# A gated-memory attention with a feed-forward layer on one core: two steps of a chunk run shifted, in three bursts of small products

## The chip, the cores and the metric

The kernel runs on one core of a Trainium2 chip. The time is that of the device from the first to the last instruction of the program, in microseconds (us). A core has a matrix engine (TensorE, PE in the profile; its weight loads are shown apart as PEld), a vector engine (VectorE, DVE), a scalar engine (ScalarE, ACT), GpSimd (POOL) and DMA queues (most of them issued by SyncE, SP). The matrix engine writes into PSUM, from where VectorE and ScalarE take the results.

## What is computed

A DeltaNet attention over 4 batches, 8 heads, 768 positions and 48 dimensions, followed by a feed-forward layer of 3072 tokens, 384 to 2048 to 384, with a PReLU between the two products. All is in float32.

```python
# attention, per batch and head; k_n is k divided by its norm
for t in range(S):
    kt, vt, bt = (k_n[:, :, t], v[:, :, t], beta[:, :, t, None])
    y[:, :, t] = np.einsum('bhd,bhde->bhe', q[:, :, t], state)
    v_old = np.einsum('bhde,bhd->bhe', state, kt)
    state = state + bt[:, :, :, None] * np.einsum('bhd,bhe->bhde', kt, vt - v_old)
# ... y becomes x, one row of 384 per token, and then
h = x @ w_in
g = np.maximum(h, 0.0) + alpha * np.minimum(h, 0.0)
out = g @ w_out
```

## The kernel before

The 768 positions are cut into 12 chunks of C = 64. A chunk is worked on in two steps of two batches each (16 matrices: 8 heads, two batches one above the other on the 128 partitions), so there are N = 24 steps; step n belongs to chunk n // 2. NJ is 4, G is 4 (pairs of heads), D is 48. Within a chunk the recurrence is solved by the inverse of a triangular 64 x 64 matrix per head and batch. Its two 32 x 32 blocks on the diagonal are inverted by elimination on VectorE, four steps (two chunks) at a time, and the part between them comes from two rounds of products (`between_1`, `between_2`).

```python
def flip(src, p):                       # q or k to the other side, two heads at a time
    for g in range(G):
        nc.tensor.transpose(
            p[:, g * 128 : (g + 1) * 128],
            src[:, 2 * g : 2 * g + 2].rearrange("p h d -> p (h d)"),
            ident,
        )
# heads lie 64 apart in src (48 values and 16 zeros each), so columns 112 to 127 are zeros

def grams(n):                           # k k^T of a later step
    p = ps_big()[:, :, 0 : G * C].rearrange("p a (g i) -> p a g i", g=G)
    for g, a, t in quarters():          # 16 products
        nc.tensor.matmul(
            p[half(t), a, g], k_t[n][dims(a), g, half(t)], k_t[n][dims(a), g, half(t)]
        )
    # ... two weighted evacuations by VectorE, into the blocks for elimination and into right[n]

def eliminate(m):                       # a generator: 39 or 43 pieces, each some VectorE operations
    # ... for j in range(1, HB - 1): prod = r * r; r = r + prod; yield

def through_state(n):
    p = ps_big()[:, :, 0 : G * (D + C)].rearrange("p a (g e) -> p a g e", g=G)
    for g, a, t in quarters():
        nc.tensor.matmul(
            p[half(t ^ a), a, g], k_t[n][dims(a), g, half(t)], beside[bp][dims(a), t, g]
        )
    p_y = ps_big()[:, :, 0 : G * D].rearrange("p a (g d) -> p a g d", g=G)
    for g, a, t in quarters():
        nc.tensor.matmul(
            p_y[half(t), a, g], q_t[n][dims(a), t, g], state[bp][dims(a), t, g]
        )
    # ... r = v - p by VectorE in three operations, the masked products of q and k, y by ScalarE
```

`solve` multiplies the inverse by r and gives u; `outputs` adds the masked products times u to y; `next_state` subtracts k times u from the state. Each of these, and of `between_1` and `between_2`, is 16 products of 48 to 64 rows and columns into a buffer of its own, followed at once by its evacuation. `ps_big` has three buffers of two banks of PSUM each; two more banks, `ffn_banks`, are the feed-forward layer's, used in turn.

One step of the attention, and how it is put among the products of the feed-forward layer:

```python
def attention(n):
    place(n + 1, (0,))
    through_state(n)
    between_1(n + 1)
    yield
    solve(n)
    grams(n + EARLY)
    between_2(n + 1)
    scale_v(n + 1)
    yield
    outputs(n)
    next_state(n)
    load_late(n + 2)
    squares(n + EARLY + 1)
    yield
    flips(n + EARLY + 1, n + 2)
    to_ffn(n)
    # ... loads of later steps
    yield

for n in range(NJ, N):
    gens = [(attention(n), SHARES), (placing(n + 1, (1, 2, 3)), SHARES * PLACING)]
    if n % NJ == 0 and n < N - NJ:
        m = n // NJ + 1
        blocks, left = eliminate(m), WHOLE + (PIECES if m > 2 else 0)
        share = -(-left // 3)
    if n % NJ < 3 and n < N - NJ:
        gens.append((part(blocks, share), share))
    if n < NJ + 2:
        gens.append((part(late, (OUT_PARTS - few) // 2), (OUT_PARTS - few) // 2))
    else:
        parts = IN_PARTS - 4 if n % 2 == 0 else FAST_PARTS + 4
        gens.append((part(tail, parts), parts))
    # ... sums of weights in steps 5, 6 and 7
    weave(*gens)
```

`weave` deals the pieces of several generators into one order of issue, evenly by the numbers given; each engine then works in that order. The feed-forward layer's two parts:

```python
def ffn_in(c):                          # 48 pieces of one product each
    for f in range(0, FT, 2):
        # ... 6 products of 256 columns into one of the two banks (L840)
        nc.scalar.activation(g, p_h, ACT.Relu, scale=-1.0)               # L850
        for i in range(2):
            nc.vector.scalar_tensor_tensor(                              # L852
                out=g[:, i], in0=g[:, i], scalar=al_t[:, f + i : f + i + 1], in1=p_h[:, i],
                op0=ALU.mult, op1=ALU.add,
            )
        # ... sums of operands for the second layer by VectorE (L794)

def ffn_out_fast(c):                    # 28 pieces of two products each
    # ... 7 groups of 8 products of 192 columns (L904), each evacuated by L924
```

Lines that the profile names: 355 transposes of q and k, 392 `grams`, 399 its evacuations, 477 and 483 elimination, 641 `between_1`, 656 `between_2`, 682 and 687 `through_state`, 707 `solve`, 720 `outputs`, 736 `next_state`, 742 the state's update, 751 transposes of y.

Of the kernel before, what the change touches and what calls it, by code (L numbers as in the profile page):

```python
# [28 lines left out]
ALU = mybir.AluOpType  # L29
# [12 lines left out]
def kernel(  # L42
# [50 lines left out]
    NXT = 2  # L93

# [258 lines left out]
    def flip(src, p):  # L353
        for g in range(G):
            nc.tensor.transpose(  # L355
                p[:, g * 128 : (g + 1) * 128],
                src[:, 2 * g : 2 * g + 2].rearrange("p h d -> p (h d)"),
                ident,
            )

    def flips(n_k, n_q):
# [13 lines left out]
        for dst, src in copies:  # L375
            nc.scalar.copy(dst.rearrange("p g i -> p (g i)"), src)  # L376
        if n_q < N:
            nc.scalar.copy(  # L378
                q_t[n_q].rearrange("p t g i -> p g t i"),
                p_q.rearrange("p (g t i) -> p g t i", g=G, t=2),  # L380
            )
# [4 lines left out]
    def grams(n):  # L386

        if n >= N:
            return
        p = ps_big()[:, :, 0 : G * C].rearrange("p a (g i) -> p a g i", g=G)  # L390
# [5 lines left out]
        for dst, cols in (  # L396
            (gather(n), slice(0, HB)), (right[n % EARLY][:, 1:], slice(HB, C))
        ):
# [4 lines left out]
        keep(n)  # L403
# [231 lines left out]
    def between_1(n):  # L635

        if n >= N:
            return
        p = ps_big()[:, :, 0 : G * HB].rearrange("p a (g i) -> p a g i", a=2, g=G)
        for g, a, t in quarters():  # L640
# [5 lines left out]
        nc.scalar.copy(  # L646
            mid[n % 2].rearrange("p (a g) i -> p a g i", a=2)[:, :, :, 0:HB], p
        )

    def between_2(n):  # L650
        if n >= N:
            return
        p = ps_big()[:, :, 0 : G * HB].rearrange("p a (g i) -> p a g i", a=2, g=G)
# [8 lines left out]
        nc.vector.tensor_tensor(out=to, in0=to if changes(n) else own, in1=p, op=ALU.add)  # L662
# [12 lines left out]
    def through_state(n):  # L675
        c, bp = steps[n]
        if c == 0:
            rhs_[n] = by_parity(nv[n])
            return
        p = ps_big()[:, :, 0 : G * (D + C)].rearrange("p a (g e) -> p a g e", g=G)  # L680
# [4 lines left out]
        p_y = ps_big()[:, :, 0 : G * D].rearrange("p a (g d) -> p a g d", g=G)  # L685
# [7 lines left out]
        for to, own, a in (  # L693
            (slice(0, 128), slice(0, 128), 0), (half(0), half(1), 1), (half(1), half(0), 1)
        ):
# [3 lines left out]
        masked(n, p[:, :, :, D : D + C])  # L699
        y = work.tile([128, H, D], FP32, name="y")  # L700
        nc.scalar.copy(by_parity(y), p_y)  # L701
        rhs_[n], ys[n] = r, y

    def solve(n):
        p = ps_big()[:, :, 0 : G * D].rearrange("p a (g d) -> p a g d", a=2, g=G)
# [5 lines left out]
        nc.vector.tensor_tensor(  # L711
            out=us[n], in0=p,
            in1=stats[n][1][:, 0:3:2, :, None].to_broadcast([128, 2, G, D]), op=ALU.mult,
        )

    def outputs(n):
        c, bp = steps[n]
        p = ps_big()[:, :, 0 : G * D].rearrange("p a (g d) -> p a g d", a=2, g=G)
# [4 lines left out]
        if c == 0:  # L723
            ys[n] = work.tile([128, H, D], FP32, name="y")
            nc.scalar.copy(by_parity(ys[n]), p)
        else:
            nc.vector.tensor_tensor(
                out=by_parity(ys[n]), in0=by_parity(ys[n]), in1=p, op=ALU.add
            )

    def next_state(n):
        c, bp = steps[n]
        if c < NCH - 1:
            p = ps_big()[:, :, 0 : G * D].rearrange("p t (g d) -> p t g d", g=G)
# [5 lines left out]
            for a in range(2):  # L740
                x = state[bp][dims(a)]
                nc.vector.tensor_tensor(out=x, in0=x, in1=p[dims(a)], op=ALU.subtract)

# [231 lines left out]
    SHARES = 4  # L975

    def attention(n):


        place(n + 1, (0,))  # L980
        through_state(n)
        between_1(n + 1)
        yield
        solve(n)
        grams(n + EARLY)
        between_2(n + 1)
        scale_v(n + 1)
        yield
        outputs(n)
        next_state(n)  # L990
# [331 lines left out]
```

## Time and profile before

| | |
|---|---|
| median of three runs | 686.55 us (684.96 to 688.63) |
| span of the profiled execution | 683.6 us |
| TensorE busy | 660.0 us, 97% |
| VectorE busy | 471.3 us, 69% |
| ScalarE busy | 249.4 us, 36% |
| products of the feed-forward layer's first part (L840) | 1152 records, 268.8 us |

The page cuts the span into 40 slices and gives each engine's busy share in tenths. TensorE has single slices below 8 only at the very start; PEclk, the granted clock of TensorE, is full in all slices. The chain of work that ended last spends 79% of the span on TensorE, 13% on VectorE and 3% on ScalarE. A matrix product in float32 appears in the trace as two records, a transpose as one. The groups by line give the busy time of a group (overlapping records counted once), the mean length of a record and the idle time of the engine ahead of it.

### The profile page before, as it was taken

To read this page: it belongs to the slowest core of one execution; us is meant where nothing else is said; L and a number is where in the kernel's file an instruction comes from. 1 tells how busy PE (TensorE), PEld (TensorE's weight loads), DVE (VectorE), ACT (ScalarE), POOL (GpSimd) and SP (SyncE) were. 2 spreads that over 40 slices of the span, in tenths; PEclk is the share of its full clock that TensorE was granted. 3 is DMA by queue.
4 is the path that set the end of the run, shared out by engine and by line. 5 is a ranking of instruction groups with operands and counts; after the bars stand their busy time and mean duration, and the time that the engine had idled before them with its cause. 6 is when DMAs were issued, how large, how long until landed. Compare 5 with 4: busy or idle time off the path is not lost.

```text
span 683.6 us, 21618 instructions
## 1 busy us (share of the span) xinstructions
PE 660.0 (97%) x9359; PEld 570.2 (83%) x9359; DVE 471.3 (69%) x1162; ACT 249.4 (36%) x586; POOL 27.8 (4%) x95
## 2 busy tenths in 40 slices
PE   5989999999889999999999999999999999999997
PEld 4567777666678988988988988988989989989997
DVE  4966789879998379978479978379877255345261
ACT  4836756344434234235235235134034133231110
POOL 5000121000000000000000000000000000000000
PEclk9999999999999999999999999999999999999999
DMA  8847644211402112112112202201201211100000
GB/s 126 236 116 218 166 106 117 70 36 37 83 18 43 34 40 48 34 39 47 35 40 36 36 25 36 37 25 36 47 18 33 53 24 20 36 1 2 23 1 24
DMA packets 110958, 37.68 MB, mean 55 GB/s; under 512 B 104160, under 2 KB 107248, under 8 KB 110864
## 3 DMA queue, kind: packets, MB, share of 16 engines
q1 hardware_dynamic: 109088, 35.81, 24.0%
q8 instruction: 74, 1.21, 0.7%
q10 hardware_dynamic: 1776, 0.49, 0.4%
q14 instruction: 20, 0.16, 0.1%
HBM read 31.56 MB, written 4.72 MB: 53 GB/s over the span
## 4 chain that ended last, share of the span: by engine, by line
PE 79%; DVE 13%; ACT 3%; issue 1%; DMA 1%; SPq 1%; POOL 0%; ACTq 0%; DVEq 0%
PE p_ffn L840 32%; PE p_ffn L904 27%; PE p_big L355 3%; DVE block L483 2%; DVE prod L477 2%; PE p_big L682 2%; PE p_big L720 2%; PE p_big L707 2%; PE p_big L641 2%; PE p_big L1009 2%; DVE act L852 1%; PE p_big L656 1%; PE p_big L392 1%; PE p_big L687 1%; DMA ke<-in_k_dram 1%
## 5 line engine op out<-in xcount | busy, mean ns | idle before, releaser
L840 PE MATMUL p_ffn<-xt,w_in 128*128 128x256 f32 x1152 | 268.8, 385 | 6.2 <-DVE act L852 2.4
L840 PEld LDWEIGHTS p_ffn<-xt,w_in 128*128 128x128 f32 x1152 | 211.9, 190 | 37.0 <-issue 4.0
L852 DVE SCALAR_TENSOR_TENSOR act<-act,al_t,p_ffn 128x256 f32<-128x256 f32 x176 | 76.3, 475 | 56.8 <-ACT act L850 55.8
L850 ACT ACTIVATE act<-p_ffn 128x512 f32<-128x512 f32 x88 | 52.4, 596 | 129.7 <-PE p_ffn L840 120.1
L904 PE MATMUL p_ffn<-w_out,act 128*128 128x192 f32 x480 | 84.2, 329 | 0.3 <-DVE act L852 0.3
L904 PEld LDWEIGHTS p_ffn<-w_out,act 128*128 128x128 f32 x480 | 78.5, 190 | 1.9 <-DVE act L852 0.9
L483 DVE TENSOR_TENSOR block<-block,prod 128x30 f32<-128x30 f32 (+9 forms) x150 | 49.8, 332 | 5.2
L477 DVE TENSOR_TENSOR prod<-block 128x30 f32<-128x30 f32 (+9 forms) x150 | 48.9, 326 | 2.0
L924 DVE TENSOR_TENSOR o_sb<-u,p_ffn 128x192 f32<-128x192 f32 x40 | 13.2, 352 | 41.4 <-PE p_ffn L904 35.1
L378 ACT COPY beside<-p_big 128x512 f32<-128x512 f32 x24 | 14.0, 589 | 54.2 <-PE p_big L355 54.2
L376 ACT COPY k_t<-p_big 128x512 f32<-128x512 f32 x24 | 13.9, 580 | 51.6 <-PE p_big L355 51.5
L701 ACT COPY y<-p_big 128x384 f32<-128x384 f32 x22 | 10.5, 478 | 57.3 <-PE p_big L687 57.3
L904 PE MATMUL p_ffn<-space_out,sums 128*128 128x192 f32 x160 | 29.3, 326 | 0.0
L904 PE MATMUL p_ffn<-more,sums 128*128 128x192 f32 x160 | 29.3, 326 | 0.0
L696 DVE TENSOR_TENSOR r<-v_raw,p_big 64x192 f32<-64x192 f32 (+1 forms) x66 | 23.2, 352 | 7.3 <-PE p_big L682 6.2
L904 PE MATMUL p_ffn<-w_out,sums 128*128 128x192 f32 x160 | 27.7, 326 | 0.0
L904 PEld LDWEIGHTS p_ffn<-space_out,sums 128*128 128x128 f32 x160 | 26.6, 190 | 0.0
L904 PEld LDWEIGHTS p_ffn<-more,sums 128*128 128x128 f32 x160 | 26.6, 190 | 0.0
L441 ACT COPY same<-right 32x256 f32<-32x256 f32 x29 | 11.7, 402 | 40.1 <-DVE right L399 39.9
L904 PEld LDWEIGHTS p_ffn<-w_out,sums 128*128 128x128 f32 x160 | 25.8, 190 | 0.0
L924 DVE TENSOR_TENSOR u<-u,p_ffn 128x192 f32<-128x192 f32 x20 | 7.1, 354 | 26.4 <-PE p_ffn L904 26.3
L609 ACT ACTIVATE diag<-inverse,which 64x128 f32<-64x128 f32 (+2 forms) x60 | 24.2, 405 | 2.2 <-DVE inverse L453 1.3
(156 smaller groups left out, 948.5 us busy)
## 6 DMA issues: line engine op xcount, KB each, us to landing
w_out<-in_moe_w_in_dram SPq DMA_DIRECT2D x12, 512.0 KB, 5.0
qp<-in_q_dram SPq DMA_DIRECT2D x48, 96.0 KB, 2.9
v_raw<-in_v_dram SPq DMA_DIRECT2D x48, 96.0 KB, 2.9
kl<-in_k_dram SPq DMA_DIRECT2D x96, 48.0 KB, 2.4
out_dram<-o_sb SPq DMA_DIRECT2D x92, 48.0 KB, 1.6
space_out<-in_moe_w_out_dram SPq DMA_DIRECT2D x11, 384.0 KB, 4.3
ke<-in_k_dram SPq DMA_DIRECT2D x43, 96.0 KB, 3.1
w_out<-in_moe_w_out_dram SPq DMA_DIRECT2D x5, 384.0 KB, 3.6
```

What stands on the lines that cost most here:

```text
L355: nc.tensor.transpose(p[:, g * 128 : (g + 1) * 128], src[:, 2 * g : 2 * g + 2].rearrange("p h d -> p (h d)"), ident,)
L376: nc.scalar.copy(dst.rearrange("p g i -> p (g i)"), src)
L378: nc.scalar.copy(q_t[n_q].rearrange("p t g i -> p g t i"), p_q.rearrange("p (g t i) -> p g t i", g=G, t=2),)
L477: nc.vector.tensor_tensor(out=prod, in0=r[:, 0:j, j : j + 1].to_broadcast([128, j, n]), in1=r[:, j : j + 1, j + 1 : HB].to_broadcast([128, ...
L483: nc.vector.tensor_tensor(out=r[:, 0:j, j + 1 : HB], in0=r[:, 0:j, j + 1 : HB], in1=prod, op=ALU.add)
L609: nc.scalar.mul(out, x, which[rows, i : i + 1])
L696: nc.vector.tensor_tensor(out=r[to, a], in0=v_in[to, a], in1=p[own, a, :, 0:D], op=ALU.subtract)
L840: nc.tensor.matmul(p_h[:, i], w_in[:, t, (f + i) * 128 : (f + i + 1) * 128], xt[:, t], start=(t == 0), stop=(t == KT - 1),)
L850: nc.scalar.activation(g, p_h, ACT.Relu, scale=-1.0)
L852: nc.vector.scalar_tensor_tensor(out=g[:, i], in0=g[:, i], scalar=al_t[:, f + i : f + i + 1], in1=p_h[:, i], op0=ALU.mult, op1=ALU.add,)
L904: nc.tensor.matmul(p, x(i), w(i), start=(i == 0), stop=(i == FP - 1))
L924: nc.vector.tensor_tensor(out=to, in0=x, in1=p, op=ALU.add)
```

## The change

The steps of a chunk, an even one (e) and an odd one (o), no longer run one after the other but shifted by a part. What each of the two needs next is put into a common burst: three bursts per chunk instead of three per step. The products of a burst share buffers of PSUM (each takes a range of columns), and their evacuations are no longer issued with the products but handed back as a list of small functions, which `lasting` and `weave` spread over the feed-forward products that follow. `between_1` and `between_2` of a step move to earlier bursts. The transposes of q and k load 112 columns, leaving out the zeros at the end, and write 112 partitions; the copies behind them and the filling products `busy` follow suit. The elimination of the diagonal blocks is dealt over both chunks that it is for, where it stood in three of four steps. It is for TensorE: fewer changes between small and full products, smaller loads, and a more even VectorE.

```diff
+    ROWS = C + D
     def flip(src, p):
         for g in range(G):
             nc.tensor.transpose(
-                p[:, g * 128 : (g + 1) * 128],
-                src[:, 2 * g : 2 * g + 2].rearrange("p h d -> p (h d)"),
+                p[0:ROWS, g * 128 : (g + 1) * 128],
+                src[:, 2 * g : 2 * g + 2].rearrange("p h d -> p (h d)")[:, 0:ROWS],
                 ident,
             )
 ...
-    def solve(n):
-        p = ps_big()[:, :, 0 : G * D].rearrange("p a (g d) -> p a g d", a=2, g=G)
+    def solve(n, p=None):
+        p = region(p, G * D, g=G)
         for g, a, t in quarters():
             nc.tensor.matmul(
                 p[half(t ^ a), a, g], inv[n % NE][half(t), a * G + g], rhs_[n][half(t), a, g]
             )
         us[n] = work.tile([128, 2, G, D], FP32, name="u")
-        nc.vector.tensor_tensor(
+        return [lambda: nc.vector.tensor_tensor(
             out=us[n], in0=p,
             in1=stats[n][1][:, 0:3:2, :, None].to_broadcast([128, 2, G, D]), op=ALU.mult,
-        )
+        )]
 ... (the other products likewise)
-    def attention(n):
- ...
+    WY = G * D
+    def ends(n, p):
+        return outputs(n, p[:, :, 0:WY]) + next_state(n, p[:, :, WY : 2 * WY])
+
+    def burst_1(c):
+        e, last = 2 * c, 2 * c - 1
+        pieces = []
+        b = ps_big()
+        if e < N:
+            p, y = ps_big(), ps_big()
+            pieces += through_state(e, p[:, :, 0 : G * (D + C)], y[:, :, 0:WY])
+            pieces += between_2(e, b[:, :, 2 * WY : 2 * WY + G * HB])
+            pieces.append(lambda: load_v(e + 3))
+        if last > NJ:
+            pieces += ends(last, b)
+            pieces.append(lambda: load_late(last + 2))
+        return pieces
+
+    def burst_2(c):
+        e, o = 2 * c, 2 * c + 1
+        b, p, y = ps_big(), ps_big(), ps_big()
+        pieces = solve(e, b[:, :, 0:WY])
+        pieces += through_state(o, p[:, :, 0 : G * (D + C)], y[:, :, 0:WY])
+        pieces += between_2(o, b[:, :, WY : WY + G * HB])
+        pieces += grams(e + EARLY, y[:, :, WY : WY + G * C])
+        pieces += [lambda: load_v(o + 3), lambda: squares(o + EARLY)]
+        return pieces
+
+    def burst_3(c):
+        e, o = 2 * c, 2 * c + 1
+        a, b = ps_big(), ps_big()
+        pieces = solve(o, a[:, :, 0:WY])
+        pieces += between_1(o + 2, a[:, :, WY : WY + G * HB])
+        pieces += ends(e, b)
+        pieces += between_1(e + 2, b[:, :, 2 * WY : 2 * WY + G * HB])
+        pieces += grams(o + EARLY)
+        pieces += [lambda: load_late(e + 2), lambda: squares(e + EARLY + 2)]
+        return pieces
 ...
     def prelude(n):
         place(n)
+        place(n + 1, (0,))
         yield
-        between_1(n)
+        now(between_1(n))
+        now(between_1(n + 1))
         yield
-        between_2(n)
+        scale_v(n)
         yield
-        scale_v(n)
+        now(burst_1(n // 2))
         yield
 ...
-    for n in range(NJ, N):
- ...
+    def stretch(n, blocks, share, *gens):
+        gens = list(gens) + [(part(tail, n), n), (part(blocks, share), share)]
+        weave(*[x for x in gens if x[1] > 0])
+    def lasting(pieces, n):
+        return each(pieces), n * len(pieces)
+    SHORT, LONG = (4, 4, 3, 3, 3, 3), (13, 15, 15, 13, 10, 10)
+    SHARES = {2: (2, 3, 3, 3, 4, 4), 3: (6, 7, 7, 4, 5, 5)}
+    EVEN, ODD = (2, 2, 3, 4, 5, 5), (0, 4, 4, 4, 5, 5)
+    for c in range(2, NCH):
+        e, o = 2 * c, 2 * c + 1
+        count = SHORT if c == 2 else LONG
+        share = SHARES.get(c, ODD if c % 2 else EVEN)
+ ...
+        stretch(count[0], blocks, share[0], (placing(o, (1, 2, 3)), 8))
+        pieces = burst_2(c)
+        stretch(count[1], blocks, share[1], lasting(pieces, 2), *early_sums)
+        turn_2(c)                       # transposes of k and q, norms, loads
+        stretch(count[2] - 2, blocks, share[2])
+ ... (in odd chunks the elimination of the next two chunks begins here)
+        place(e + 2, (0,))
+        place(o + 2, (0,))
+        stretch(2, blocks, 0)
+        pieces = burst_3(c)
+        n = count[3] // 2
+        stretch(n, blocks, 0 if c % 2 else share[3] // 2, lasting(pieces, 1))
+        stretch(
+            count[3] - n, blocks, share[3] if c % 2 else share[3] - share[3] // 2, *late_sums
+        )
+        to_ffn(e)
+        scale_v(e + 2)
+        stretch(count[4], blocks, share[4], (placing(e + 2, (1, 2, 3)), 7))
+        pieces = burst_1(c + 1)
+        stretch(count[5], blocks, share[5], lasting(pieces, 2))
+        turn_1(c + 1)                   # transposes of k, q and y, norms, loads
```

## The prediction, made before the changed kernel was timed

> **What bounds the kernel now.** First the page's busy rows, to find the engine, then the busy time by stretch, to find where it is the bound.
>
> ```profile
> PE 660.0 (97%) x9359; PEld 570.2 (83%) x9359; DVE 471.3 (69%) x1162; ACT 249.4 (36%) x586; POOL 27.8 (4%) x95
> ```
>
> ```profile
> 150.00:217.00 67.00, 61.19 (x1103) 46.20 (x1100) 60.49 (x151) 29.03 (x75) 2.94 (x10) 1.00 0.26 49
> 217.00:250.00 33.00, 33.00 (x509) 31.02 (x508) 18.81 (x41) 11.03 (x30) 0.41 (x2) 1.00 0.19 38
> 250.00:650.00 400.00, 399.65 (x5334) 364.21 (x5333) 266.92 (x646) 123.27 (x288) 3.04 (x14) 1.00 0.16 31
> ```
>
> The columns after the stretch and its length are TensorE, its weight loads, VectorE, ScalarE and GpSimd. From 217 us to the end TensorE never stops (399.65 of 400.00 us): there a microsecond taken off its stream is a microsecond off the time, and a microsecond taken off VectorE (267 of 400) is worth nothing. From 150 to 217 us, which holds chunk 2 and half of chunk 3, TensorE is idle for 5.8 us and VectorE is busy for 60.5 of 67: VectorE is nearly the bound there.
>
> Busy is not the same as useful, so next the chain of work in order of time, one step of the attention in the steady part. Its columns are start, length (from the end of the piece before) and the number of records; an issued product shows as two records, a transpose as one.
>
> ```profile
> 300.26 0.44 PE p_big L656 x32
> 300.70 5.38 PE p_ffn L840 x24
> 306.07 0.61 PE p_big L720 x32
> 306.69 0.36 PE p_big L736 x32
> 307.05 4.95 PE p_ffn L840 x22
> 311.99 0.87 PE p_big L355 x8
> 312.87 0.33 PE p_big L751 x3
> 313.19 4.32 PE p_ffn L840 x20
> 317.51 0.93 PE p_big L682 x32
> 318.44 0.45 PE p_big L687 x32
> ```
>
> The reader is to compare pieces of one line by what stands before them. L840 after transposes: 4.32 us for 20 records, 0.216 each. L840 after small products: 5.38 for 24, where 24 x 0.216 is 5.18, and 4.95 for 22, where 22 x 0.216 is 4.75. So the return from small products to full ones costs 0.20 us, and the return from transposes nothing. The way in costs too: L720, first of its burst, takes 0.61 us; L656 and L687, which also load 64 columns per record but follow other small products, take 0.44 and 0.45. That is 0.15 us or more. One burst of small products costs **0.35 us beside the products in it**, whatever it holds.
>
> [...] all small products here work on 48 or 64 rows and columns, and 0.35 us is lost around each burst of them, none around transposes, which use all 128 rows. [...]
>
> ```profile
> L720 PEld LDWEIGHTS p_big<-u,a_t 64*64 64x64 f32 x384 | 6.7, 134 | 3.3 <-issue 3.1 <-DVE prod L477 0.2
> L736 PEld LDWEIGHTS p_big<-u,kl 64*48 64x48 f32 x384 | 5.5, 122 | 0.0
> ```
>
> 16 columns less make a load 12 ns shorter, and in the chain L736 (48 columns loaded) takes 0.36 us where groups with 64 columns take 0.44. [...]
>
> **The change, part by part.**
>
> *Bursts.* Before, each of the 20 steps from 4 to 23 has three bursts (state products with the first half of the next step's inverse; solve, Gram products and second half; outputs and new state), so 60, and the prelude has two: 62. After, the prelude has two (both first halves; burst 1), and each of the 10 chunks three: 32. The products are the same. 30 bursts less at 0.35 us are 10.5 us of TensorE time. Not all of it stands on the path: about 24 of the 30 lie after 217 us, 24 x 0.35 = **8.4 us**. The other 6 (2.1 us) fall into the stretch where VectorE is close to full; I count a third, **0.7 us**.
>
> *Transposes.* 188 of q and k load 112 columns in place of 128. 92 of them (60 of q, 32 of k by the line's count) come after 217 us. At 12 to 13 ns each that is 1.2 us, if the load sets the pace. If streaming does, it is nothing: L840 moves 256 columns in 0.216 us, so 128 columns at that rate would take 0.108 us, also what is seen. The trace of before can't tell. I take two chances in three, **0.8 us**. The copies behind them keep their 512 elements per partition and take what they took.
>
> *Inversion spread.* In chunks 2 and 3, elimination runs 13 blocks per step over three steps; after, 19 blocks stand in chunk 2 and 20 in chunk 3. So chunk 2 has 7 blocks (of some 0.8 us of VectorE) less, and chunk 3 up to its deadline 7 more. Total VectorE work up to the deadline near 217 us is unchanged, so little of the 5.8 us of idle TensorE can come back: I take **1.0 us**, since the waits for u and y in chunk 2 (0.4 and 1.5 us) should go. After 217 us TensorE doesn't wait and spreading is worth nothing by itself.
>
> *What is added.* No instruction. But evacuations of five or six products now come in one packet, and two banks of the feed-forward must be freed among them. After burst 3 of an even chunk VectorE has, between one pair of L852 and the next: one update of the state 0.55, two elimination pairs 0.8 each, L399 twice 0.41, an operand sum 0.69, a norm 0.55: 4.2 us. With 0.6 for the relu, 0.87 for the first pair and 0.48 for the first half of the second, the last operand of the second layer is ready 6.15 us after the burst's own bank is full. TensorE comes to need it after 12 records of 0.216 and 14 of 0.1625: 4.9 us. That would be a new wait of 1.2 us, in chunks 4, 6 and 8; in odd chunks the elimination is not there and it fits. Three such waits are 3.7 us; my order of work on VectorE is from the program, the moments are not, so I take less than half, **minus 1.5 us**.
>
> Sum: 8.4 + 0.7 + 0.8 + 1.0 - 1.5 = 9.4 us; 686.55 - 9.4 = 677.2, which I round to **677.0 us**.
>
> **The rivals.** (a) *The waits eat the gain.* A burst of 3 us with three double buffers of PSUM at once, products of one burst in the same banks, and packets of eight VectorE operations[...]. For it: the reckoning above, where the slack of a feed-forward bank is only about 1 us (2.6 us to fill the other one, less 0.6 and 0.87). Against: VectorE is full to 67% in the steady part, and before the change its packets of u, two Gram evacuations, the inverse and v (0.55 + 0.41 + 0.41 + 0.41 + 0.55) already stood in the same way, with only 0.35 us of idle TensorE in 400. A wait of 1.2 us in each of nine chunks would leave the time near 682.
> (b) *The cost of a burst is not fixed but goes with its length or the kinds in it.* A longer burst changes between products with different rows and columns more often. Then merging saves less, perhaps only the 0.20 us on the way out: 24 x 0.2 and the small terms make 681. Against: L687 after L682 and L656 after L392 show no extra.
> (c) *VectorE's stretch gains more than I give.* All of its 5.8 us of idle time and the whole of the 2.1 us there come back, and transposes pay in full: 671. For it: the shares of elimination look chosen for that stretch. Against: 60.5 us of VectorE work in 67.
>
> **Range and chances.** The firm part is 8.4 us, good to 15% (0.30 to 0.40 us a burst). The soft terms run from minus 4 (rival a) to plus 6 (rival c). The range is 671.5 to 682.5 us. Over 2% would need 672.8, so 13.7 us: only rival (c) nearly whole gets there, one chance in ten. Slower by over 2% would need 23 us of new waits; 0.02. Within 2%: 0.88.
>
> **What would show it.** In the chain after, full products behind transposes should keep 0.216 us, and those behind a burst carry 0.20 more, with three such places in a chunk instead of six; L700 (the old L682), where it is second in burst 2, should take about 0.78 us in place of 0.93. Eight transposes of k and q should take 0.77 us if loads set the pace, 0.87 if streaming does. Idle TensorE from about 217 us to the end should be under 4 us, and stand at L932 for act. If it is above 6, rival (a) is right; if a burst's overhead grows with its length, rival (b). The prediction fails if the number of bursts is not what sets that 0.35 us.

## The result, and the profile after

The changed kernel takes **707.08 us** (706.32 to 711.49, median of 4 runs); the kernel before, run beside it, takes 685.94. The ratio is **1.032 [1.027, 1.036]**: slower by 3%, where 677.0 was predicted, and outside the range of 671.5 to 682.5.

The row of busy time of the changed kernel:

```profile
PE 658.8 (94%) x9359; PEld 573.0 (81%) x9359; DVE 466.6 (66%) x1162; ACT 247.8 (35%) x586; POOL 29.5 (4%) x95
```

The numbers of instructions are the same on every engine, and the busy times changed by less than 5 us. So nothing was added to the work; TensorE stands idle for longer. Where, the busy time by stretch tells (columns as in the prediction; the last four are the granted clock, the DMA share and GB/s, after GpSimd):

```profile
150.00:194.00 44.00, 36.23 (x725) 25.51 (x726) 34.85 (x89) 19.31 (x53) 3.12 (x8) 0.92 0.28 52
194.00:217.00 23.00, 19.71 (x239) 16.73 (x239) 19.93 (x51) 7.91 (x19) 0.41 (x2) 1.00 0.27 52
217.00:250.00 33.00, 31.13 (x499) 28.94 (x498) 26.32 (x65) 9.71 (x24) 0.00 (x0) 1.00 0.11 22
250.00:650.00 400.00, 383.70 (x5321) 351.93 (x5320) 255.98 (x621) 123.55 (x295) 4.53 (x16) 1.00 0.16 31
```

From 250 to 650 us TensorE was idle for 0.35 us before and is now for 16.3. From 150 to 217 it is idle for 11.1 us in place of 5.8, and for once its clock was not full (0.92).

A finer table has the time from the first L840 (now L868) of one chunk's feed-forward to that of the next. "Pass 2" ends where the feed-forward of chunk 2 begins, at 194.5 us after the change, and pass 3 starts there:

```
pass              before   after   difference
start to pass 2    95.2     96.6     +1.4
2                  92.3     97.9     +5.6
3                  55.1     56.7     +1.7
4 to 8            254.6    269.7    +15.1
9 to the end      186.5    183.7     -2.8
whole span        683.6    704.6    +21.0
```

Passes 9 and 10 are the change as it was meant: 48.38 us each where before had 49.37 and 49.38. The loss stands in passes 2 to 8, which are those in which the inversion's elimination still runs on VectorE (its last operation, L498, starts at 517.5 us). The waits of TensorE in the changed kernel (total, times, longest, in us):

```profile
PE p_ffn L932 <- DVE act L880: 8.0, 6, 2.1
PE p_big L779 <- DVE y L749: 6.0, 1, 6.0
...
PE p_ffn L868 <- DVE act L880: 3.9, 3, 1.3
PE p_big L656 <- issue: 2.9, 3, 1.2
PE p_ffn L868 <- ACT norm L340: 2.5, 2, 1.2
```

The kernel before has for the same three groups (L840 is now L868, L904 is L932, L751 is L779):

```profile
PE p_ffn L840 <- DVE act L852: 2.4, 3, 1.2
PE p_big L751 <- DVE y L727: 1.5, 1, 1.5
PE p_ffn L904 <- DVE act L852: 0.3, 2, 0.2
```

I counted from 150 us on what each piece of the chain took beyond its usual pace. Before: 7.5 us. After: 34.1 us, of which 8.9 is L932 waiting for act, 8.5 is L868 behind the transposes of the second stretch, 7.8 is L779's wait for y with the slower clock behind it, 4.2 is stops in the middle of a burst, 1.7 is L932 for o_sb and 1.5 is L656 for diag. Against this stands the gain of the merged bursts, some 10 us. That leaves +16.6, where passes 2 to the end show +19.6: the count, or the estimate of the gain, misses 3 us. TensorE's idle time needs no such estimate: it rises by 22.9 us in passes 2 to 8 and not at all behind them, while its busy time falls by 0.5 us there and by 2.8 us from pass 9 on, +19.6 in all.

**One such wait, read closely.** In pass 5, two queues stand in the way. First ScalarE, in order of time (start, length, instruction; in brackets the idle time before it and what ended it):

```profile
315.89 0.60 ACT L878 ACTIVATE act<-p_ffn 128x512 f32<-128x512 f32 x1 [5.93 <-PE p_ffn L868]
316.38 0.47 ACT L723 COPY y<-p_big 128x384 f32<-128x384 f32 x1
319.98 0.81 ACT L456 COPY same<-right 32x256 f32<-32x256 f32 x2 [3.12 <-DVE right L409]
320.82 0.52 ACT L330 ACTIVATE ksq<-ke 128x384 f32<-128x384 f32 x1
321.25 1.07 ACT L878 ACTIVATE act<-p_ffn 128x512 f32<-128x512 f32 x2
```

L456 copies a part of `right`, which VectorE has not yet taken out of PSUM. ScalarE's instructions run here in the order of issue, so it stands for 3.12 us, and behind the copy stand a square (L330) for which everything is there, and two relus (L878) whose banks filled meanwhile. Then VectorE in the same stretch:

```profile
313.92 0.70 DVE L715 TENSOR_TENSOR r<-v_raw,p_big 128x192 f32<-128x192 f32 x2
316.52 0.87 DVE L880 SCALAR_TENSOR_TENSOR act<-act,al_t,p_ffn 128x256 f32<-128x256 f32 x2 [1.90 <-ACT act L878]
317.42 0.35 DVE L715 TENSOR_TENSOR r<-v_raw,p_big 64x192 f32<-64x192 f32 x1
...
319.54 0.41 DVE L409 TENSOR_TENSOR right<-p_big,wgt 128x256 f32<-128x256 f32 x1
321.38 0.55 DVE L332 TENSOR_REDUCE norm<-ksq 128x8 f32<-128x384 f32 x1 [1.43 <-ACT ksq L330]
```

The products of burst 2 were done between 312.5 and 314.4 us. But the change spreads their evacuations over the feed-forward, and so the third of r, the mask, the inverse and `right` stand in the queue behind L880, which can't start until its own bank is full and the relu has run: VectorE is idle for 1.90 us, with five operations behind L880 whose products are done. `right` comes at 319.54, releases ScalarE, which releases VectorE's norm (L332), which stands ahead of the next L880: and only then, at 323.25, does TensorE get a bank for L868, after 1.35 us of standing still. Two queues hold each other up in turn.

Before, the same copy stood in ScalarE's queue and waited for VectorE as well (L441, in the step that the prediction shows):

```profile
301.18 0.82 ACT L441 COPY same<-right 32x256 f32<-32x256 f32 x2 [2.19 <-DVE right L399]
```

But there VectorE took `right` directly behind the burst, at 300.74 us, and in that pass TensorE was not idle at all.

### The profile page after: what moved, and what is told of

The parts are those of the page before. It is cut to its first block, busy times and chain, and to the rows that moved or that the text cites. A ratio compares the mean times of both kernels' runs of the same rounds, so it can differ in the third digit from the quotient of the medians.

```text
span 704.6 us, 21576 instructions
## 1 busy us (share of the span) xinstructions
PE 658.8 (94%) x9359; PEld 573.0 (81%) x9359; DVE 466.6 (66%) x1162; ACT 247.8 (35%) x586; POOL 29.5 (4%) x95
## 4 chain that ended last, share of the span: by engine, by line
PE 72%; DVE 16%; ACT 5%; issue 3%; DMA 2%; SPq 1%; POOL 0%; ACTq 0%; DVEq 0%
PE p_ffn L868 30%; PE p_ffn L932 22%; DVE act L880 2%; PE p_big L700 2%; PE p_big L730 2%; PE p_big L356 2%; DVE prod L492 2%; PE p_big L656 2%; PE p_big L670 2%; DVE block L498 2%; PE p_big L743 2%; PE p_big L1059 2%; DVE block L468 1%; PE p_big L705 1%; PE p_ffn L910 1%
## 5 line engine op out<-in xcount | busy, mean ns | idle before, releaser
L868 PE MATMUL p_ffn<-xt,w_in 128*128 128x256 f32 x1152 | 265.4, 384 | 11.8 <-DVE act L880 3.9
L868 PEld LDWEIGHTS p_ffn<-xt,w_in 128*128 128x128 f32 x1152 | 213.8, 190 | 43.0 <-ACT act L878 7.0
L880 DVE SCALAR_TENSOR_TENSOR act<-act,al_t,p_ffn 128x256 f32<-128x256 f32 x176 | 75.9, 473 | 78.1 <-ACT act L878 77.9
L878 ACT ACTIVATE act<-p_ffn 128x512 f32<-128x512 f32 x88 | 51.9, 595 | 163.9 <-PE p_ffn L868 158.1
L932 PE MATMUL p_ffn<-w_out,act 128*128 128x192 f32 x480 | 84.4, 328 | 8.0 <-DVE act L880 8.0
L932 PEld LDWEIGHTS p_ffn<-w_out,act 128*128 128x128 f32 x480 | 78.0, 190 | 10.2 <-DVE act L880 9.7
L498 DVE TENSOR_TENSOR block<-block,prod 128x30 f32<-128x30 f32 (+9 forms) x150 | 49.8, 332 | 5.2
L332 DVE TENSOR_REDUCE norm<-ksq 128x8 f32<-128x384 f32 x24 | 13.0, 550 | 24.6 <-ACT ksq L330 24.5
L932 PE MATMUL p_ffn<-space_out,sums 128*128 128x192 f32 x160 | 29.3, 327 | 0.0
L932 PE MATMUL p_ffn<-more,sums 128*128 128x192 f32 x160 | 29.3, 326 | 0.0
L734 DVE TENSOR_TENSOR u<-p_big,wgt 128x384 f32<-128x384 f32 x24 | 13.4, 557 | 22.3 <-PE p_big L670 19.6
L932 PE MATMUL p_ffn<-w_out,sums 128*128 128x192 f32 x160 | 27.6, 326 | 0.0
L377 ACT COPY k_t<-p_big 112x512 f32<-112x512 f32 x24 | 13.9, 580 | 38.8 <-PE p_big L356 38.6
L932 PEld LDWEIGHTS p_ffn<-space_out,sums 128*128 128x128 f32 x160 | 26.5, 190 | 0.1
L932 PEld LDWEIGHTS p_ffn<-more,sums 128*128 128x128 f32 x160 | 26.6, 190 | 0.0
L932 PEld LDWEIGHTS p_ffn<-w_out,sums 128*128 128x128 f32 x160 | 26.3, 190 | 0.0
L379 ACT COPY beside<-p_big 112x512 f32<-112x512 f32 x24 | 14.0, 590 | 32.0 <-PE p_big L356 31.9
```

The lines of the kernel that those rows point to most:

```text
L498: nc.vector.tensor_tensor(out=r[:, 0:j, j + 1 : HB], in0=r[:, 0:j, j + 1 : HB], in1=prod, op=ALU.add)
L868: nc.tensor.matmul(p_h[:, i], w_in[:, t, (f + i) * 128 : (f + i + 1) * 128], xt[:, t], start=(t == 0), stop=(t == KT - 1),)
L880: nc.vector.scalar_tensor_tensor(out=g[:, i], in0=g[:, i], scalar=al_t[:, f + i : f + i + 1], in1=p_h[:, i], op0=ALU.mult, op1=ALU.add,)
L932: nc.tensor.matmul(p, x(i), w(i), start=(i == 0), stop=(i == FP - 1))
```

## The experiments

My theory after reading the traces: the time goes to *order in two queues*, ScalarE's (L456) and VectorE's (spread evacuations). The rivals: the elimination in its new place overloads VectorE; the rows of the transposes or the clock; the length of a burst itself. Ratios below are to the kernel before.

### Is it the elimination?

In both kernels the multiply and add of the elimination are left out from chunk 2 on, so the results are not those of the reference; the times show what this work of VectorE costs each order.

```diff
+            if m > 1:
+                yield
+                continue
```

> Leaves out the multiply and add of each elimination from chunk 2 on (its transposes stay), so the output is not the reference's. Theory 1 (the elimination pieces in VectorE's queue make the new waits): the waits at L932 for act and those behind the transposes of burst 2's stretch vanish, TensorE is idle under 3 us from 217 us on, time about 671 us, 10 us under the kernel before with the same left out. Theory 2 (the spread evacuations themselves stand behind feed-forward operations that cannot start yet, in VectorE's and in ScalarE's queue): most of the 19 us of waits at these two places stays, time above 685 us, no better than the kernel before with the same left out.

> The kernel before with the same left out. Both theories: TensorE is the bound from 217 us on, so nothing changes there; only the 5.8 us of idle TensorE between 150 and 217 us can come back, time 680 to 683 us. It is the base for the run after_no_elim.

After without it: 691.92 us, 1.008 [1.006, 1.010]. Before without it: 681.35 us, 0.993 [0.990, 0.995]. So the elimination costs the old order 5 us and the new one 15. But without any of it the new order is still slower than the old by 10.6 us, and L868 and L932 (here L871 and L935) still wait for act, 10.5 us in all:

```profile
PE p_ffn L871 <- DVE act L883: 6.3, 6, 1.4
PE p_ffn L935 <- DVE act L883: 4.2, 5, 1.5
```

Half of the loss needs the elimination, half doesn't: neither theory has all of it. For pass 2 it is the whole: 89.0 us after and 89.7 before.

### Evacuations in one packet, and the copies off ScalarE

One kernel issues the evacuations of a burst at once, ahead of the feed-forward that follows:

```diff
-        stretch(count[1], blocks, share[1], lasting(pieces, 2), *early_sums)
+        now(pieces)
+        stretch(count[1], blocks, share[1], *early_sums)
 ... (bursts 3 and 1 likewise)
```

> The changed kernel with the evacuations of each burst issued in one packet right behind its products, not spread over the feed-forward products that follow. Theory 1: no change, 704 to 710 us, since the same elimination pieces stand in the same stretches. Theory 2: VectorE no longer idles 2 us for L880 with evacuations behind it; the waits at L932 and behind the transposes fall to less than half, time under 698 us.

The other leaves them spread, and moves the copies of L456 to GpSimd:

```diff
-            if n < FIRST + NJ and n != NJ - 1:
+            if n >= NJ or n != NJ - 1:
                 nc.gpsimd.tensor_copy(out=same[m][own, j], in_=right[n % EARLY][own, 1:])
```

> The changed kernel with the copies L456 (of the Gram products into the blocks for elimination) on GpSimd, so that ScalarE no longer waits for L409 with two L878 behind them. Theory 1: no change, 704 to 710 us. Theory 2, if ScalarE's queue is the part that counts: the waits behind the transposes (8.5 us) vanish and those at L932 shrink, 696 to 700 us; if VectorE's queue alone counts: within 2 us of 707.

The packet alone: 709.03 us, 1.033 [1.028, 1.038], no gain, which by itself is what the rival theory expected; the waits for act only change place, from L932 (8.0 to 3.3 us) to L868 (3.9 to 12.3). The copies alone: 695.50 us, **1.013 [1.009, 1.018]**, 11.6 us less than the changed kernel. Of five waits of L868 behind the transposes of the second stretch one is left (2.6 us), and L932's for act fall from 8.0 to 5.9 us. The same place in the step, on ScalarE, with the copies on GpSimd:

```profile
310.59 0.52 ACT L330 ACTIVATE ksq<-ke 128x384 f32<-128x384 f32 x1
312.19 0.60 ACT L878 ACTIVATE act<-p_ffn 128x512 f32<-128x512 f32 x1 [1.08 <-PE p_ffn L868]
314.78 0.60 ACT L878 ACTIVATE act<-p_ffn 128x512 f32<-128x512 f32 x1 [1.99 <-PE p_ffn L868]
```

The square and the relus now wait only for their own inputs, and TensorE has no wait behind the transposes that follow. ScalarE, at 35% busy, had looked as if it couldn't matter. With ScalarE held up, the packet has nothing to give. With both:

> The changed kernel with both: evacuations in one packet right behind the burst, and the copies L456 on GpSimd. If the packet alone did nothing because ScalarE's queue held L878 behind L456 anyway, it should now pay: the waits at L932 for act (1.1 to 1.5 us in six chunks of after_pool) go, time 688 to 690 us. If a packet only moves the wait (L880 now stands behind eight evacuations), within 2 us of after_pool's 695.5, with the waits at L868.

690.79 us, **1.007 [1.005, 1.009]**: another 4.7 us. In passes 4 to 8 the waits for act fall from 4.9 to 3.2 us, and from L932 mostly to L868; those of L932 for o_sb (0.8 us) go, and passes 2 and 3 gain too. So the packet helps, but only once ScalarE's queue is clear, and in part it moves the wait.

### Pass 2: dealing, order, sums

What is left of pass 2's loss is the wait of L779 for y. On VectorE, in the changed kernel:

```profile
184.82 0.41 DVE L492 TENSOR_TENSOR prod<-block 128x238 f32<-128x238 f32 x1
185.26 0.41 DVE L498 TENSOR_TENSOR block<-block,prod 128x238 f32<-128x238 f32 x1
185.59 0.35 DVE L715 TENSOR_TENSOR r<-v_raw,p_big 128x192 f32<-128x192 f32 x1
...
188.84 0.41 DVE L498 TENSOR_TENSOR block<-block,prod 128x240 f32<-128x240 f32 x1
189.17 0.55 DVE L749 TENSOR_TENSOR y<-y,p_big 128x384 f32<-128x384 f32 x1
```

VectorE doesn't stop between 182.7 and 190. y of step 5 (L749) comes out of the shared burst 1 now, behind the r, mask and inverse of step 6 and the elimination woven among them, and TensorE has only 20 pieces of feed-forward in all of chunk 2 to fill the time. It was idle for 6.0 us and then worked at a granted clock of 0.50 from 186.5 to 193.3 us. The clock fell 2.8 us into the stop. In the kernel with the copies on GpSimd the same wait is one of 4.9 us, and the granted clock is 1.00 from 180 to 185 us, 0.66 from 185 to 190 and 1.00 again from 190; behind a stop of 2.5 us, at 208.9 us here, it is 1.00. The records behind the wait of 6.0 us took some 1.6 us longer than theirs in the kernel before. The attempts on this wait:

> after_pool with the elimination's pieces in chunk 2 dealt 5, 5, 5, 2, 1, 1 over its six stretches in place of 2, 3, 3, 3, 4, 4. If the 5.1 us wait for y at the end of chunk 2 comes from four pieces each in stretches of three feed-forward products: it vanishes, with 1.6 us of half clock behind it, 689 us. If VectorE is simply full up to the deadline in chunk 3: the wait moves to chunk 3, above 693 us.

Its edit, on top of the copies on GpSimd, gives chunk 2's first stretches more elimination and the last ones less:

```diff
-    SHARES = {2: (2, 3, 3, 3, 4, 4), 3: (6, 7, 7, 4, 5, 5)}
+    SHARES = {2: (5, 5, 5, 2, 1, 1), 3: (6, 7, 7, 4, 5, 5)}
```

697.22 us, 1.016 [1.011, 1.021]. Pass 2 takes 94.3 us as it did (94.5): the wait at 190 shrinks to 2.4 us and one of 1.7 comes at 179, still in chunk 2. The whole is no faster than the 695.50 us without it (the intervals overlap): moving work inside a full queue moved the wait.

> after_now_pool with y and the state ahead of the next step's evacuations in burst 1, and no elimination piece in the seven feed-forward pieces behind burst 2 and the six behind burst 3. If the waits left in chunks 4 to 8 (1.1, 1.1, 0.7, 0.4 and 0.6 us) come from elimination standing beside the packets, they go; y of chunk 2 comes 2.5 us earlier. Time 684 to 687 us, about as before the change. If VectorE has no room at all there, 690.

```diff
-            pieces += ends(last, b)
+            pieces = ends(last, b) + pieces
 ... (packets and GpSimd's copies as above)
-    SHARES = {2: (2, 3, 3, 3, 4, 4), 3: (6, 7, 7, 4, 5, 5)}
-    EVEN, ODD = (2, 2, 3, 4, 5, 5), (0, 4, 4, 4, 5, 5)
+    SHARES = {2: (2, 3, 3, 3, 4, 4), 3: (6, 7, 7, 3, 5, 5)}
+    EVEN, ODD = (4, 2, 4, 2, 5, 5), (0, 3, 5, 3, 5, 5)
 ... (no elimination in the first 6 or 7 pieces behind bursts 2 and 3)
```

695.35 us, 1.012 [1.007, 1.017], above both expectations and no better than the two edits alone. In passes 4 to 8 no wait for act is left (3.2 us with the two edits alone), but y first in its packet did not bring pass 2 back: L779 now waits for the mask (a_t, 4.6 us) that must clear a bank, and L932 gets a new wait for u of up to 0.6 us a chunk. A wait was turned into others.

> after_best with the eight sums of weights (0.95 us each) on GpSimd in place of VectorE, all of them due between 150 and 225 us. If that stretch is bound by VectorE's work, 3 to 6 us less than after_best, 679 to 682 us, below the kernel before. If its waits are a matter of order alone, within 1 us of after_best.

> The kernel before with its sums of weights on GpSimd. It has 5.8 us of idle TensorE in the stretch from 150 to 217 us; if VectorE's work is the bound there, 2 to 5 us come back, 681 to 684 us; if not, 685 to 686.

```diff
-            nc.vector.tensor_tensor(   (the sums of weights)
+            nc.gpsimd.tensor_tensor(
```

698.68 us, 1.018 [1.015, 1.021], and for the kernel before 691.15 us, 1.007 [1.005, 1.009]. Taking work from the full engine made the kernel before slower and the changed one no faster (its interval overlaps that of 695.35 us). Why, VectorE shows in the kernel before with GpSimd's sums, which start at 168.87 us and take 1.8 to 2.3 us each:

```profile
168.43 0.38 DVE L483 TENSOR_TENSOR block<-block,prod 128x210 f32<-128x210 f32 x1
168.84 0.39 DVE L477 TENSOR_TENSOR prod<-block 128x220 f32<-128x220 f32 x1
169.26 1.88 DVE L483 TENSOR_TENSOR block<-block,prod 128x220 f32<-128x220 f32 x1
171.18 1.89 DVE L477 TENSOR_TENSOR prod<-block 128x228 f32<-128x228 f32 x1
```

The same operation, on nearly as many columns, takes 0.38 us alone and 1.88 beside GpSimd. Each slowed operation ends some 0.2 us behind the end of a sum (171.14 and 173.07 us, the sums 170.91 and 172.81), so it lasts as long as the sum beside it. L852, which takes one of its inputs from PSUM, shows no slowing in its mean: 463 ns from 150 to 220 us, and 460 in the kernel before. What the two engines share the trace doesn't show.

### Transposes and clock

> One part alone: the kernel before with transposes of q and k that load 112 columns, copies of 112 partitions and filling products of 112 rows. The prediction's step (the load sets the pace of a transpose): 1 to 2.5 us less, 683 to 685 us, 0.77 us for eight transposes. What the changed kernel's trace says (0.87 us for eight as before): no gain. A further theory: the filling products of the first 50 us keep fewer rows of TensorE active, so that its clock is lowered there more often (in 7 of 10 kernels with 112 rows the trace has 3 to 24 us at half clock between 16 and 50 us, in none of three with 128): then slower by 1 to 5 us, with such a stretch in the trace.

> after_now_pool with the 128 columns and rows of before in the transposes, copies and filling products. If the 112 do nothing, within 1 us of its 690.8; if they lower the clock in the first 50 us, 2 to 4 us less and no half clock between 16 and 50 us.

The first gives the kernel before the 112 columns; the second takes them from the changed kernel with both edits (`ROWS = 128`). Before with 112: 685.41 us, 1.000 [0.998, 1.003], and eight transposes take 0.87 us as they did with 128. In its chain:

```profile
311.32 0.87 PE p_big L356 x8
```

So the load doesn't set their pace: 109 ns for 128 columns is also L840's pace (256 columns in 0.216 us), and the 112 columns are worth nothing. After with 128: 688.48 us, 1.004 [1.002, 1.006], beside 1.007 [1.005, 1.009] with 112; the intervals touch, so I don't claim a difference. I had suspected the 112 of the half clock in the first 50 us of some traces. It is absent from the first of these and present in the trace of the hybrid below, with 128; in all, 6 of 10 traces with 112 have it and 2 of 6 with 128. The granted clocks speak against it: below 0.997 in 4 of 14 executions with the 112 alone, and in 12 of 35 of the kernel before beside them. The idea fell, and what starts those stretches stays open.

### Stops inside a burst

In the changed kernel TensorE stops four times after 217 us in the middle of a burst, with nothing that it waits for (1.05, 0.63, 1.02 and 1.19 us; the count above has 0.1 us more for each). Here the kernel with both edits and 128 columns, on TensorE:

```profile
319.28 0.63 PE L656 MATMUL p_big<-diag,right 64*64 64x32 f32 x32
319.73 0.55 PE L403 MATMUL p_big<-k_t 48*64 48x64 f32 x20
321.30 0.45 PE L403 MATMUL p_big<-k_t 48*64 48x64 f32 x12 [1.02 <-issue]
```

L403 stops after 20 of its 32 records, 180 records into the burst. Each such stop comes after 150 to 180 records, and each has a transfer of 16,384 bytes on the queue of instructions (q8) close before it: in the changed kernel 274.57 to 275.53, 311.59 to 312.47, 331.34 to 332.44 and 491.16 to 492.21 us, with the stops ending at 276.94, 314.02, 333.70 and 493.49. That queue moved 74 such packets, for 18,718 products and loads of TensorE: 253 per packet, an estimate that takes all packets for TensorE's. A burst of 160 records has as many loads, so by this estimate it uses up more than a packet in some 2.5 us, where these four packets took 0.9 to 1.1 us to come and the stops ended 1.2 to 1.6 us after that. In the kernel before, the longest burst of small products in the steady part has 96 records, and in 14 of its 60 bursts after 150 us such a transfer began, without a stop for instructions. In the changed kernel's bursts of 160 and more, of 17 in which one began, four stopped. Two tests:

> after_pool with the Gram products of burst 3 taken out of it and issued three feed-forward products later, a burst of their own. If the stops of 1.0 to 1.6 us in the midst of a burst (L403 and L656, waiting for nothing that the profile shows) come from TensorE using up its instructions faster than they are fetched (after some 150 records): those of burst 3 vanish, 3 us, while 8 more bursts at 0.35 us cost 2.8, so the time stays at 694 to 697 us, and the stops in burst 2 stay. If the stops come from what the products wait for: they go on in the small burst.

```diff
-        pieces += grams(o + EARLY)          (in burst_3)
+        g = grams(o + EARLY)                (three feed-forward products later)
+            late_sums.append(lasting(g, 1))
```

Here, in odd chunks, the elimination reads the last step's blocks before the moved products have written them, so the numbers are not the reference's; the amount of work is. 697.91 us, 1.016 [1.011, 1.022]: no faster than 695.50 (the intervals overlap); the moved products make seven bursts more. The kernel that it is built on has three stops in bursts 3, after 159, 178 and 150 records. The one among the moved products is gone, and alone these products never stop; the other two (now after 159 and 151 records) stay, as does the one in a burst 2.

> after_now_pool_128 with 32 small products more in the prelude (128 instructions of TensorE[...]; their results are used nowhere). If the stops in long bursts (after 153 to 180 records, in four of the bursts after 217 us) come from fetching instructions: those four vanish and others come up in other bursts, again with a fetch 1 to 1.5 us into the burst. If they come from what these products wait for: the same four bursts stop at the same products. Time within 2 us of 688.5 in both cases.

32 more small products in the prelude, to move the place of the packets in the stream:

```diff
+        for _ in range(32):
+            nc.tensor.matmul(
+                p[half(0), 0:HB], diag[n % NE][half(0), 0], diag[n % NE][half(0), 0, 0:HB]
+            )
```

698.67 us, 1.018 [1.012, 1.023]: pass 2, where that prelude stands, got 10 us longer, far outside the 2 us expected, so the total says nothing. The trace does. Of the four bursts that stopped without them, three no longer do, and a burst 3 of chunk 7 now stops, after 156 records: 1.4 us after 217 us in place of 4.3. In the fourth, burst 3 of chunk 4, the stop comes after 96 records, where it came after 160, at L403:

```profile
268.10 0.69 PE L403 MATMUL p_big<-k_t 48*64 48x64 f32 x32 [1.09 <-issue]
```

```profile
277.90 0.53 PE L759 MATMUL p_big<-u,kl 64*48 64x48 f32 x29 [0.49 <-issue]
```

That is 64 records earlier, as many as the 32 added products have; from the start of the trace, both stops come after 4,145 records of TensorE. So a stop keeps its place in the stream of instructions, not in the work, and waiting for inputs doesn't explain it. That and the packet beside each stop fit instructions that come late; when an instruction reaches TensorE the trace doesn't show, so this stays my reading.

### The old order where VectorE is full, the new one behind it

> Chunks 2 and 3 in the old order (three bursts per step), the shifted bursts from chunk 4 on, with evacuations in one packet, L456 on GpSimd from there on, no elimination piece close behind bursts 2 and 3, and 128 columns. If the loss of chunks 2 and 3 comes from the shift in a stretch where VectorE is full: up to the start of chunk 4's burst 2 it runs as before the change, and then gains 1 us per chunk less the stops in bursts: 680 to 683 us, below the kernel before. If the bursts themselves lose time wherever they stand: 686 or more.

```diff
+    def attention(n): ...                   (the steps of before, for chunks 2 and 3)
+    for n in range(NJ, NJ + 3): ...
-    for c in range(2, NCH):
+    for c in range(4, NCH):
 ... (packets, GpSimd's copies, 128 columns, shares as in the order experiment)
```

684.32 us, **0.998 [0.996, 1.000]**: a little faster than the kernel before, and 3% faster than the changed one, but 1.3 us above the range expected. The traced execution is its longest, 690.15 us, with half clock from 30 to 50.5 us; the passes behind that compare. Passes 2 and 3 are back at 92.2 and 55.2 us, as before the change, and passes 9 and 10 keep their 48.38. Passes 4 to 8 do not gain the 1 us each that was expected: they take 256.9 us, still 2.3 more than before. The gain is that of passes 9 to the end, 2.8 us. What it still waits for:

```profile
PE p_ffn L868 <- DVE act L880: 2.4, 3, 1.2
PE p_big L403 <- issue: 2.3, 2, 1.2
PE p_ffn L868 <- DVE prod L492: 1.7, 1, 1.7
PE p_big L656 <- issue: 1.5, 2, 1.3
```

The first and third stand in the kernel before as well; the stops inside bursts (issue, 3.8 us) don't. With them TensorE is idle for 5.2 us in passes 4 to 8, and its busy time falls there by 2.5 us where 5 were expected; why by half only stays open. An order that changes only from pass 9 on wasn't tried.

## Why the prediction was wrong

**The gain per burst was right, where it stands alone.** Chain of work in the changed kernel, in a step without elimination:

```profile
582.27 0.44 PE p_big L356 x4
582.71 6.48 PE p_ffn L868 x30
589.19 0.61 PE p_big L730 x32
589.80 0.45 PE p_big L656 x32
590.25 0.48 PE p_big L743 x32
...
591.54 4.08 PE p_ffn L868 x18
```

Behind transposes L868 takes 6.48 / 30 = 0.216 us a record; behind the burst 4.08 less 18 x 0.216 is 0.19; L730, first of its burst, takes 0.61 and those behind it 0.45. L700, second in burst 2, takes 0.78 as said. Passes 9 and 10 have three bursts less each and take 1.0 us less: 0.33 per burst where 0.35 was used, with bursts of up to 160 records. In passes 4 to 8 the gain can't be seen apart from the waits. Rival (b) is out as it was put, though length has a price of its own, the stops.

**The transposes** took the road that the prediction gave one chance in three: 0.87 us for eight. The term of 0.8 us is 0. The loads did get shorter, in the steady part from 141 to 134 ns, by 7 where 12 to 13 were reckoned, and the transposes did not: 109 ns for 128 columns is the pace of one record of a full product (0.216 us for 256 columns), which has two, so the gain over a product is twofold, an estimate from these two figures. That the load is what sets the pace was my estimate; no trace of before showed it.

**The failed step is "what is added", put at minus 1.5 us.** By the count above, the waits at the feed-forward's banks are 19.1 us (8.9, 8.5 and 1.7), and all new waits together some 27. The reckoning had the right place and the right kind: L932 for act behind burst 3, 1.2 us each in chunks 4, 6 and 8; the runs show six such waits of up to 2.1 us, one in each of the chunks 3 to 8, the odd ones, where it was to fit, among them. It failed in three ways. It added up VectorE's operations as if each could start when the one before it ended, but in the queue they stand behind an L880 that has to wait for its own bank. Behind burst 3 of chunk 5:

```profile
336.32 0.87 DVE L880 SCALAR_TENSOR_TENSOR act<-act,al_t,p_ffn 128x256 f32<-128x256 f32 x2 [2.91 <-ACT act L878]
337.22 0.56 DVE L767 TENSOR_TENSOR beside<-beside,p_big 48x384 f32<-48x384 f32 x1
```

```profile
342.02 0.59 PE L932 MATMUL p_ffn<-w_out,act 128*128 128x192 f32 x2 [1.51 <-DVE act L880]
```

VectorE stands for 2.91 us with half of the state's update (L767) and both L409 behind L880, though the burst was done at 334.2 us, and later L932 stands for 1.51. It followed VectorE alone, though ScalarE carries the relus and, since the copies of L456 stand in the same queue, waits for VectorE in its turn; moving those copies took 11.6 us off. And it looked at one burst of three: the waits behind the transposes of the second stretch, 8.5 us, are as large. Halving the figure because the moments were uncertain had no ground; a queue that is held up by another gets later, not earlier.

**"Chunk 2 gains 1.0 us" was wrong in sign**: pass 2 lost 5.6. The prediction saw the elimination get lighter in chunk 2, and not that the shift puts y of step 5 behind the work of step 6, while the feed-forward of chunk 2 needs it. Its own first view had the warning, 60.5 us of VectorE work in 67.

**Rival (a) was right**, in kind and by its own sign (idle TensorE above 6 us after 217; it is 18.2 from 217 to 650). It was given 682 us, with waits of 1.2 us per chunk; up to four waits per chunk came. The stops inside bursts, 4.2 us, and the half clock, 1.6, were in no rival.

Open: 3 us that the count doesn't place, and what a deeper buffer for the products of a burst would bring; that wasn't tried.

## What to carry to other kernels

Before you merge bursts on a bound engine, write down the queues of *all* engines that evacuate them, in the order of issue, and ask of each entry what it waits for and who stands behind it: an engine that is busy for a third of the time (ScalarE, 35%) held up the bound one here. Waits that cost TensorE 0.35 us in 400 with short bursts cost 16.3 with long ones. Where an engine has no room, keep the old order there and use the new one where there is room: here that was from pass 9 on, where the elimination's products are over. A gain per event that is measured well (0.33 us) says nothing about a loss that was reckoned from an order.

## What the runs showed of the hardware

- In bursts of 160 and more small records TensorE stopped in the changed kernel four times after 217 us, for 0.63 to 1.19 us, with nothing to wait for: after 150 to 180 records, each time with a transfer of 16,384 bytes on the queue of instructions close before it. In the kernel with both edits and 128 columns, 32 more products ahead made one such stop come 64 records earlier, after 96 in place of 160: at the same place in the stream of instructions. In the kernel before, with bursts of 96 or less, there is none after 150 us.
- Beside GpSimd's sums three operations of the elimination on VectorE (L477, L483) take 1.87 to 1.89 us each in place of some 0.39 in the kernel before, and each ends some 0.2 us behind the end of a sum. The sum itself takes 1.8 to 2.3 us there and 0.95 on VectorE, so the move lost twice.
- Six microseconds of idle TensorE cost 7.6: the granted clock is 0.50 for 6.8 us from the middle of the stop. Behind a stop of 4.9 us it was 0.66 for 5 us, and behind one of 2.5 us it was 1.00.
- A transpose of 128 columns takes 109 ns, whether 112 or 128 columns were loaded (loads of 134 and 141 ns).
